# The first batch of a block-sparse attention and mixer kernel: a new order of loads, casts and weights, all-row mask products, and keys at the head of ScalarE's queue

## The chip, the core and the metric

The kernel runs on one NeuronCore of a Trainium2 chip. The metric is the device time of one execution in microseconds, read as the median of several executions. The profile is of one execution; its span leaves out some 1.8 us of the metered time. Names used below: TensorE (matrix products; "PE" in profile lines, "PEld" for its weight loads), VectorE ("DVE"), ScalarE ("ACT"), GpSimd ("POOL"), SyncE ("SP"; here it only issues DMAs). A trailing q (SPq, ACTq, POOLq) marks a DMA issue.

## The reference

Four batches, eight heads, 768 positions, head size 64. Attention with a block mask (blocks of 32: neighbours, first and last block, and three sampled key blocks for each query block), then a mixer:

```python
scores = scale * q @ k^T
mask = neighbour | first/last block | sampled blocks       # 24 x 24 blocks of 32
attn = softmax(where(mask, scores, -1e9)); x = attn @ v    # x: (4, 768, 512)
h = (x^T @ U) @ V                                          # rank 32
u = x + h^T
out = u + relu(u @ w_ch1) @ w_ch2                          # 512 -> 2048 -> 512
```

## The kernel before

Work goes in 16 pairs of heads; four pairs make a batch. A pair has nine units; a unit is a score product (`psc`), one 128x1024 exponential on ScalarE (`est`), and later the value products (`pav`). Batch 0 (pairs 0 to 3, 36 units) has no dense work to overlap with. From pair 4 on TensorE interleaves attention with the two dense products (`pt`, `pch`). In batch 0 the mask is carried inside the score product: 64 extra rows of `qa` hold a mask row per block, 64 extra rows of `ka` hold a one-hot pattern. The mask rows come from a small product, here called the mask product (`pm`).

The start, cut to what the argument touches:

```python
    keep(nc.vector.memset(zeros, 0.0))
    for h in (1, 0):
        keep(nc.vector.memset(ka[0][h][mrows[h], :], 0.0))
    keep(nc.vector.memset(cbd, 0.0))
    # ... (two more memsets)
    keep(nc.sync.dma_start(out=sbi[0:NB]...,  in_=sampled_blocks...))
    keep(nc.scalar.dma_start(out=small[0:NB], in_=small_dr.ap()))              # mask constants, NB = 24 rows
    keep(nc.sync.dma_start(out=qld[:, :, 0:TQ], in_=q0[:, :, 0:TQ]))
    keep(nc.scalar.dma_start(out=kld[:, :, 0:TK], in_=k0[:, :, 0:TK]))         # first keys
    # ... rest of q0, k0, identity, one-hot patterns
    vld = new_ld(0, "v")
    keep(nc.gpsimd.tensor_copy(out=vld[:, 0, 0, 0:1], in_=kld[:, 0, 0, 0:1]))  # a gate: v0 waits for the keys
    keep(nc.sync.dma_start(out=vld, in_=src_of("v", 0)))
    issue(1)                                                                   # q1, k1, v1, behind v0 on SyncE
    warm_pe(8)                                                                 # eight 128x512 products of zeros
    # ... VectorE: eq, cb, cbd from small and sampled_blocks
    def mask_mm(o, a, e):
        mm(o, cbd[0:NB].rearrange("z a c -> z (a c)"), small[0:NB, a:e], True, True)
```

What hangs on the units of batch 0, cut in the same way:

```python
WLOADS = ...((1, 3), (1, 5), (1, 7), (2, 0), (2, 3), (2, 5), (2, 7), (3, 0))   # w1 x4, then w2 x4, from GpSimd
# after unit 0 of pair 0, on SyncE:
#   for both heads: copy of the mask rows for the second buffer, one-hot pattern (64 rows) for it
#   V, V, U, then q2, k2
# at unit 6 of pair i, on GpSimd: casts of q and k of pair i+2, before the tails (which hold the casts xh and uh)
```

"Tails" are the mixer's first steps for a finished pair: `pa`, `ph`, the GpSimd cast `uh`, and TensorE's turning of it (`puT`).

The softmax here doesn't subtract the row's maximum and nothing guards it: scores larger than these inputs give would overflow.

## Time and profile before

| | before |
|---|---|
| time, median | 283.48 us (3 runs, 282.89 to 284.21) |
| profiled span | 281.8 us |
| first exponential starts | 7.26 us |
| 37th exponential ends | 45.44 us |
| first product with w1 starts | 47.98 us |
| ScalarE busy between first and 37th | 35.32 of 38.18 us |
| TensorE busy, 78 to 203 us | 124.54 of 125.00 us |

The page's first parts, engine totals and the clock row, look as if TensorE were the limit throughout:

```profile
PE 272.5 (97%) x3497; PEld 162.3 (58%) x3497; DVE 175.1 (62%) x285; ACT 177.5 (63%) x199; POOL 100.5 (36%) x132
...
PEclk9999999999999999999999999999999999999999
```

The split by stage says otherwise. Columns of these lines: stretch and its length, then busy time and instruction count of PE, PEld, DVE, ACT and POOL, then granted clock, DMA share, GB/s.

```profile
7.26:45.44 38.18, 34.86 (x489) 25.17 (x488) 25.25 (x54) 35.32 (x37) 25.53 (x39) 1.00 1.03 261
...
78.00:203.00 125.00, 124.54 (x1851) 75.57 (x1849) 93.33 (x137) 88.81 (x97) 57.12 (x66) 1.00 1.10 106
```

In the second stretch TensorE has half a microsecond to spare in 125. In the first, ScalarE ought to be the limit, as each unit has one exponential, but it idles 2.9 us. The timeline of ScalarE in that stretch shows where (start, length, what; x7 is a run of seven, and the bracket is the idle time before the run and what ended it):

```profile
7.26 6.90 ACT L494 ACTIVATE est<-psc 128x1024 f16<-128x1024 f32 x7 [0.54 <-PE psc L174]
14.49 4.69 ACT L494 ACTIVATE est<-psc 128x1024 f16<-128x1024 f32 x5 [0.33 <-PE psc L174]
...
23.95 2.94 ACT L494 ACTIVATE est<-psc 128x1024 f16<-128x1024 f32 x3 [0.51 <-PE psc L174]
28.26 17.18 ACT L494 ACTIVATE est<-psc 128x1024 f16<-128x1024 f32 x18 [1.38 <-PE psc L174]
46.28 1.94 ACT L494 ACTIVATE est<-psc 128x1024 f16<-128x1024 f32 x2 [0.84 <-PE psc L174]
```

The chain of waits through 5 to 60 us follows the late start at 28.26 back to its cause (start, length, what):

```profile
6.35 8.04 DMA vld<-in_v_dram
...
14.45 0.84 POOL vt L242
...
15.62 6.63 DMA vld<-in_v_dram
...
22.30 0.83 POOL vt L242
...
25.07 0.83 POOL kst L248
25.91 0.45 POOL uh L655
...
27.39 0.34 PE puT L707 x3
...
28.26 0.80 ACT est L494
```

v1 lands 8.0 us after its issue, GpSimd casts it, v2 can only then be issued and lands 6.6 us later, GpSimd's casts stand in a row behind it, uh among them, and TensorE's turning of uh is what the exponential waited for.

SyncE's timeline has the cause of the late q2 (L319 is v0; L233 at 6.35 is v1, at 14.46 q2; L1002 is U):

```profile
4.91 0.37 SPq L319 DMA_DIRECT2D vld<-in_v_dram  x1
...
6.35 0.47 SPq L233 DMA_DIRECT2D vld<-in_v_dram  x1
...
12.59 0.35 SPq L1002 DMA_DIRECT2D w2t<-in_moe_U_dram  x1
14.46 0.38 SPq L233 DMA_DIRECT2D qld<-in_q_dram  x1
```

q2, issued at 14.46, waited 1.4 us for v1 to land, though its buffer had been free since 5.5.

TensorE at the start:

```profile
0.99 3.59 PE L174 MATMUL warm<-m 128*128 128x512 f16 x8 [0.99 <-DVE m L286]
4.51 0.76 PE L174 MATMUL pm<-w1t,cbd 24*128 24x512 f16 x3
5.21 0.39 PE L174 MATMUL warm<-m 128*128 128x512 f16 x1
```

The first eight products are 0.43 us apart. The same products are 0.21 us apart from 5.8 us on; the two spacings are called half and full clock below. The three mask products (512, 512 and 256 columns) after 4.51 need 0.70 us in all to the next product's start. The profile's granted clock reads 1.00 over these 7.26 us.

### The profile page before, as it was taken

The numbers are of one execution on the slowest core, as the hardware profiler recorded it, in microseconds if no ns is written. First come the engines' busy times: TensorE is split into PE (matmuls) and PEld (weight loads), VectorE is DVE, ScalarE is ACT, GpSimd is POOL, SyncE is SP. The second block draws the span as 40 slices with busy tenths as digits, with TensorE's granted clock in tenths as the row PEclk, the third lists the DMA queues.
The fourth block names the chain that finished last, engine by engine and source line by source line (L and its number), as shares of the span: only waits on it lengthen the run. The fifth ranks groups of instructions, "written<-read, shape, count | busy, mean of one in ns | idle before, by whom it ended". The sixth has DMA issues, their size and how long they took to land.

```text
span 281.8 us, 8050 instructions
## 1 busy us (share of the span) xinstructions
PE 272.5 (97%) x3497; PEld 162.3 (58%) x3497; DVE 175.1 (62%) x285; ACT 177.5 (63%) x199; POOL 100.5 (36%) x132
## 2 busy tenths in 40 slices
PE   8997998999999999999999999999999999999995
PEld 3565775456566564656665555657565544655443
DVE  6765767797888878765967767784979541000112
ACT  4997997696969847595876657596868101654000
POOL 2379857205356646361614545361102020000000
PEclk9999999999999999999999999999999999999999
DMA  5989999993979999997794999993100313000112
GB/s 173 268 240 333 238 247 187 155 117 25 95 75 112 155 122 148 139 131 83 49 123 28 142 100 134 167 111 55 30 2 2 102 22 128 31 1 2 74 74 77
DMA packets 85716, 31.71 MB, mean 112 GB/s; under 512 B 75304, under 2 KB 83312, under 8 KB 85680
## 3 DMA queue, kind: packets, MB, share of 16 engines
q0 software_dynamic: 49728, 10.10, 47.7%
q1 hardware_dynamic: 35464, 20.85, 35.0%
q8 instruction: 27, 0.44, 0.6%
q10 hardware_dynamic: 488, 0.24, 0.3%
q14 instruction: 9, 0.07, 0.1%
HBM read 27.90 MB, written 6.29 MB: 121 GB/s over the span
## 4 chain that ended last, share of the span: by engine, by line
PE 79%; DMA 6%; ACT 6%; POOL 3%; issue 2%; DVE 1%; SPq 1%; ACTq 0%; POOLq 0%; DVEq 0%
PE pt L174 29%; PE pch L174 28%; PE pav L174 10%; PE psc L174 8%; ACT est L494 6%; DMA vld<-in_v_dram 5%; PE pa L174 2%; DMA kld<-in_k_dram 1%; POOL xh L594 1%; PE ph L174 1%; POOL uh L655 1%; POOL vt L242 1%; POOL w1t L434 0%; SPq L233 0%; DVE xh L537 0%
## 5 line engine op out<-in xcount | busy, mean ns | idle before, releaser
L494 ACT ACTIVATE est<-psc 128x1024 f16<-128x1024 f32 x144 | 142.5, 1028 | 42.0 <-PE psc L174 40.4
L174 PE MATMUL pt<-uT,w1t 64*128 64x384 f16 (+1 forms) x896 | 94.6, 324 | 0.5 <-ACT est L494 0.4
L174 PE MATMUL pch<-w2t,tT 64*128 64x512 f16 (+3 forms) x688 | 93.3, 372 | 0.2
L515 DVE TENSOR_TENSOR est<-est,m 128x1024 f16<-128x1024 f16 x108 | 78.7, 745 | 17.2 <-ACT est L494 16.0
L174 PEld LDWEIGHTS <-w1t 64*128 64x128 f16 (+1 forms) x896 | 46.7, 94 | 36.5 <-PE pt L174 6.7
L174 PEld LDWEIGHTS <-tT 64*128 64x128 f16 (+1 forms) x688 | 37.7, 95 | 38.5 <-PE pch L174 1.4
L732 ACT ACTIVATE tT<-pt 128x768 f16<-128x768 f32 (+1 forms) x48 | 36.8, 776 | 33.7 <-PE pt L174 33.7
L174 PEld LDWEIGHTS <-est 128*128 128x128 f16 x1152 | 41.4, 97 | 10.9 <-issue 5.1
L174 PE MATMUL pav<-vt,est 128*128 128x65 f16 x1152 | 44.4, 193 | 0.1
L594 POOL CAST xh<-xs 128x768 f16<-128x768 f32 x12 | 11.5, 955 | 86.5 <-DVE xs L585 55.9
L787 DVE TENSOR_TENSOR of<-xf,pch 128x1024 f32<-128x1024 f32 (+3 forms) x16 | 15.3, 954 | 43.5 <-PE pch L174 43.4
L174 PE MATMUL psc<-qT,kT 64*128 64x512 f16 (+1 forms) x288 | 40.8, 323 | 0.0
L680 POOL CAST uh<-xf 128x768 f16<-128x768 f32 x12 | 13.0, 1087 | 25.2 <-issue 12.9
L174 PE MATMUL psc<-qa,ka 128*128 128x512 f16 (+1 forms) x96 | 21.5, 326 | 0.3
L734 DVE TENSOR_SCALAR tT<-pt 128x768 f16<-128x768 f32 (+1 forms) x20 | 18.2, 916 | 4.6 <-PE pt L174 4.5
L174 PEld LDWEIGHTS <-kT 64*128 64x128 f16 x288 | 14.4, 94 | 11.0 <-DVE xs L585 0.2
L262 POOL DMA_DIRECT2D qst<-in_q_dram x20 | 16.3, 821 | 0.1
L262 POOL DMA_DIRECT2D vt<-in_v_dram x20 | 16.3, 822 | 0.0
L262 POOL DMA_DIRECT2D kst<-in_k_dram x20 | 16.3, 821 | 0.0
L583 DVE RECIPROCAL rcp<-pav 128x12 f32<-128x12 f32 x12 | 2.8, 233 | 16.0 <-PE pav L174 16.0
L585 DVE TENSOR_TENSOR xs<-pav,rcp 128x768 f32<-128x768 f32 x12 | 11.5, 958 | 1.2
L671 DVE TENSOR_TENSOR xf<-xs,ph 128x768 f32<-128x768 f32 x12 | 11.4, 950 | 1.3 <-PE ph L174 1.1
(68 smaller groups left out, 134.8 us busy)
## 6 DMA issues: line engine op xcount, KB each, us to landing
out_dram<-of SPq DMA_DIRECT2D x9, 512.0 KB, 3.7
vld<-in_v_dram SPq DMA_DIRECT2D x6, 384.0 KB, 8.0
w1t<-in_moe_w_ch_dram POOLq DMA_DIRECT2D x4, 512.0 KB, 10.7
w2t<-in_moe_w_ch_dram POOLq DMA_DIRECT2D x4, 512.0 KB, 18.4
qld<-in_q_dram SPq DMA_DIRECT2D x5, 384.0 KB, 6.2
kld<-in_k_dram SPq DMA_DIRECT2D x5, 384.0 KB, 7.2
qst<-in_q_dram POOLq DMA_DIRECT2D x20, 96.0 KB, 3.9
kst<-in_k_dram POOLq DMA_DIRECT2D x20, 96.0 KB, 4.8
```

Source lines behind the costliest of these rows:

```text
L174: ins = nc.tensor.matmul(out, lhsT, rhs, start=start, stop=stop, skip_group_check=loose)
L242: nc.gpsimd.tensor_copy(out=vts[b % 2][:, 2 * hp : 2 * hp + 2, :, 0:D], in_=ld)
L262: keep(nc.gpsimd.dma_start(out=o[:, h], in_=src_of(nm, i)[:, h]))
L494: keep(nc.scalar.activation(out=est, in_=psc, func=AF.Exp, scale=0.125))
L515: keep(nc.vector.tensor_tensor(out=o, in0=o, in1=m, op=ALU.mult))
L585: nc.vector.tensor_tensor(out=xs.rearrange("p (c j) (h d) -> p c (j h) d", c=2, h=2), in0=pv[:, :, :, 0:D], in1=rcp[:, :, :, None].broadca ...
L594: keep(nc.gpsimd.tensor_copy(out=xh, in_=xs))
L671: nc.vector.tensor_tensor(out=u.rearrange("p (c j) n -> p c j n", c=2), in0=xs.rearrange("p (c j) n -> p c j n", c=2), in1=ph[:, :, 0:HS]. ...
L680: keep(nc.gpsimd.tensor_copy(out=uh, in_=u))
L732: keep(nc.scalar.activation(out=o, in_=i, func=AF.Relu))
L734: keep(nc.vector.tensor_scalar_max(out=o, in0=i, scalar1=0.0))
L787: nc.vector.tensor_add(out=of, in0=xfs[b][:, sc : sc + nsc, n0:n1], in1=pch)
```

## The change

Its intent: bring the loads, casts and weights of batch 0 into the order in which they are needed, start the keys first, and run the mask products over all 128 rows. The core of the diff (cut where marked):

```diff
     keep(nc.vector.memset(zeros, 0.0))
+    keep(nc.vector.memset(small, 0.0))
@@ issues at the start
-    keep(nc.scalar.dma_start(out=small[0:NB], in_=small_dr.ap()))
     keep(nc.sync.dma_start(out=qld[:, :, 0:TQ], in_=q0[:, :, 0:TQ]))
     keep(nc.scalar.dma_start(out=kld[:, :, 0:TK], in_=k0[:, :, 0:TK]))
+    keep(nc.scalar.dma_start(out=small[0:NB], in_=small_dr.ap()))
@@ mask_mm
-            cbd[0:NB].rearrange("z a c -> z (a c)"),
-            small[0:NB, a:e],
+            cbd.rearrange("z a c -> z (a c)"),
+            small[:, a:e],
@@ GpSimd, after the casts of pair 0 (the memsets of the ones column move to the very start)
-    for vt in vts:
-        keep(nc.gpsimd.memset(vt[:, :, :, D : D + 1], 1.0))
+    for h in range(2):
+        hot_rows(nc.gpsimd, 1, h, D)          # was on SyncE, between the mask-row copies
@@ SyncE after unit 0 of pair 0
-   V, V, U, q2, k2
+   q2, U, k2, V, V
@@ weights
-            ((1, 3), (1, 5), (1, 7), (2, 0), (2, 3), (2, 5), (2, 7), (3, 0))
+            ((1, 3), (1, 4), (2, 3), (2, 4), (HP, 0), (HP, 2), (HP, 4), (HP, 6))
@@ casts of the next pair, now after the tails
-        if u == 6:
-            cast(i + 2, "q")
-            cast(i + 2, "k")
-        if u == 8:
-            cast(i + 2, "v")
         for _ in range(...): tails.popleft()()
+        if u == 7:
+            cast(i + 2, "q")
+        if u == 8:
+            cast(i + 2, "k")
+        if u == 0 and i > 1:
+            cast(i + 1, "v")
```

Also, pair 2 is turned one unit earlier and its q is cast before U.

More of the change, by code (lines that the diff above doesn't have):

```diff
@@ L314 @@
     keep(nc.scalar.activation(out=dummy, in_=zeros[:, 0:1], func=AF.Exp))
+    for vt in vts:
+        keep(nc.gpsimd.memset(vt[:, :, :, D : D + 1], 1.0))
     vld = new_ld(0, "v")
@@ L989, in at_unit @@
                     mask_rows("dve", h, pm2[:, 0, 0:QB], QA, S)
+                for nm, o, pt, t in (("q", qa[0], pq, TQ), ("k", ka[0], pk, TK)):
+                    for h in range(2):
+                        half_copy(nc.vector.tensor_copy, o, h, pt, t, T)
+                for h in range(2):
                     keep(
@@ L994, in at_unit @@
                     )
-                    hot_rows(nc.sync, 1, h, D)
-                for nm, o, pt, t in (("q", qa[0], pq, TQ), ("k", ka[0], pk, TK)):
-                    for h in range(2):
-                        half_copy(nc.vector.tensor_copy, o, h, pt, t, T)
-                for h in range(2):
-                    keep(nc.sync.dma_start(out=mvld[h * R : h * R + R], in_=moe_V))
+                issue(2, "q")
                 keep(
@@ L1005, in at_unit @@
                 )
-                issue(2, "qk")
+                issue(2, "k")
+                for h in range(2):
+                    keep(nc.sync.dma_start(out=mvld[h * R : h * R + R], in_=moe_V))
                 cast(1, "q")
@@ L1014, in at_unit @@
             if u == 6:
+                cast(2, "q")
                 cast_U()
-                cast(2, "q")
                 cast(2, "k")
@@ L1034, in at_unit @@
             WLOADS[i, u]()
-        at = u - 2 if i == 1 else u - 1
-        if at in range(4):
-            turn_part(i + 1, "qk"[at // 2], at % 2)
-        if u == 6:
-            cast(i + 2, "q")
-            cast(i + 2, "k")
-        if u == 8:
-            cast(i + 2, "v")
+        if u in (1, 2, 3, 4):
+            turn_part(i + 1, "qk"[(u - 1) // 2], (u - 1) % 2)
         for _ in range({0: 1, 5: 2, 6: 1, 7: 1}.get(u, 0)):
@@ L1069, in unit_sides @@
             turn_dma(i + 1, "k")
+        if (i, u) in WLOADS:
+            WLOADS[i, u]()
         if u in (3, 5, 7):
@@ L1104 @@
             flush_value()
+            cast(HP + 1, "v")
         if gi == 1:
```

## The prediction

> **What bounds it now.** Batch 0 (first 45 us, 36 units) runs at ScalarE's pace: one 128x1024 exponential per unit; in the undisturbed stretch (timeline, 28.3 to 45.4 us) 18 take 17.2 us, 0.955 us each. After about 48 us TensorE is the limit: 79.7 us busy of 80 between 120 and 200 us (windows). So whatever brings stage two forward reaches the end undiluted; nothing else counts.
>
> Stage one loses time. The timeline shows ScalarE idle for 0.33, 0.29, 0.51 and 1.38 us before exponentials between 14 and 28 us, then 0.84 at 46.3. The chain of waits explains them: 26.7% of 5 to 60 us is value loads (v of pair 1: 8.0 us from issue; pair 2: 6.6), then GpSimd casts that queue behind them, then TensorE waiting for GpSimd's uh cast (0.40+0.65 us near 27). Again later: the cast of k of pair 5 waits 2.8 us for a load that took 17.4 us, delays uh, and TensorE waits at 44.8.
>
> **What the change does.**
> - SyncE's queue: [...] Before, U waits for k1 (issued 12.6), q2 for v1 (14.5, though its buffer was free at 5.5). After, the two 96 KB pattern loads leave that queue and q2 leads U and V: q2 should issue near 8.5, k2 near 9, about 5 us earlier.
> - w2 (4 x 512 KB) moves from 30-37 us to the first units of pair 4, near 40-48. In 25 to 45 us the software queue takes 79.7% of the DMA engines, the hardware queue 29.6%. [...] Loads of pairs 4 and 5 should land in under 10.
> - GpSimd: uh now precedes the casts of the next pair (0.83 us each). The two added pattern issues (0.6 us each on SyncE) fit the 0.8 us idle before the first v cast plus the 0.53 us memset that moves earlier.
> - Start: a 128x408-word memset (0.38 us for 128x384), the keys' load 0.6 us earlier, the mask constants' 0.6 later. The mask products start when the eight warming products end (4.5 us), not when cbd is ready (3.4); that slack hides both. All-row products stream the same columns.
> - TensorE's order changes only in when pair 2's q and k are turned (one unit earlier); ScalarE's compute order not at all.
>
> **Sum.** Exponential gaps: 2.5 us, of which 0.4 stay (q2 and q3 turns have less slack behind GpSimd). Transition at 44 to 47 us: 0.7. Start: 0.1. Stage two gives back 0.2: q6/k6 loads stand behind two or three w2 pieces in the software queue; needed near 71 us, first w2 use near 79. Net 2.7 us of 283.5, 1%.
>
> Predicted 280.8 us, 279.4 to 282.6 eight times in ten. Faster by over 2%: 0.03; within: 0.95; slower: 0.02.
>
> **What would show it.** ScalarE's gaps between 14 and 28 us shrink from 2.5 to under 0.7; the 36th exponential ends near 42 (was about 44.5); first product with w1 near 45 (was 48.0); q2 issued before 9.5; k5 lands in under 10 us; w2 landed before 70; TensorE's idle from 50 to 200 us unchanged (under 1 us); first exponential near 7.2.
>
> **What would make it wrong.** k6 arriving after 65 us, so pair 6's scores stall (up to 2 us); GpSimd's order putting q2, U, k2 behind a late v1; late mask constants moving the first exponential past 7.6; pair 5's transposing DMAs, now meeting w2, taking over 15 us.

What the trace of before shows is that U waited 1.9 us for k1 to land and q2 1.4 us for v1, and that k5 took 17.4 us to land where the quickest load of keys took 3.3. The sum came to 2.1 + 0.7 + 0.1 - 0.2 = 2.7 us. That k5 would land in under 10 us once w2 had moved, on which part of the transition's 0.7 rests, is the author's estimate.

## The result

The changed kernel takes 280.78 us (median of 4 runs, 280.53 to 280.88) against 283.62 (4 runs, 282.89 to 284.21). The ratio is 0.990, 95% interval 0.9875 to 0.9924. Ratios here are the mean time of one kernel's fast runs over the mean of the other's of the same rounds, so not quite the ratio of the medians quoted. The change is about 1% faster, and the interval is clear of 1.

```profile
PE 272.3 (98%) x3497; PEld 162.6 (58%) x3497; DVE 175.4 (63%) x286; ACT 177.0 (63%) x199; POOL 101.7 (36%) x134
...
PEclk9999999999999999999999999999999999999999
```

The split by stage, with boundaries at the same events as before (same columns):

```profile
8.19:43.20 35.01, 34.63 (x499) 25.47 (x497) 25.53 (x55) 34.88 (x37) 22.61 (x35) 1.00 0.90 243
...
75.00:200.00 125.00, 124.54 (x1855) 75.58 (x1853) 93.33 (x138) 88.68 (x97) 56.99 (x66) 1.00 1.08 106
```

ScalarE's exponentials, before in six runs with gaps, are now two:

```profile
8.19 35.01 ACT L497 ACTIVATE est<-psc 128x1024 f16<-128x1024 f32 x37 [0.54 <-PE psc L174]
43.42 1.94 ACT L497 ACTIVATE est<-psc 128x1024 f16<-128x1024 f32 x2 [0.22 <-PE psc L174]
```

SyncE (L322 is v0; L233 at 5.36 is v1, at 9.29 q2; L1004 is U):

```profile
3.29 0.37 SPq L322 DMA_DIRECT2D vld<-in_v_dram  x1
...
5.36 0.48 SPq L233 DMA_DIRECT2D vld<-in_v_dram  x1
...
9.29 0.55 SPq L233 DMA_DIRECT2D qld<-in_q_dram  x1
9.89 0.49 SPq L1004 DMA_DIRECT2D w2t<-in_moe_U_dram  x1
```

v0 goes 1.6 us earlier, v1 1.0, q2 5.2. TensorE at the start:

```profile
0.99 3.59 PE L174 MATMUL warm<-m 128*128 128x512 f16 x8 [0.99 <-DVE m L286]
4.78 1.25 PE L174 MATMUL pm<-w1t,cbd 128*128 128x512 f16 x3 [0.20 <-DVE cbd L353]
5.82 0.63 PE L174 MATMUL warm<-m 128*128 128x512 f16 x1
6.25 0.50 PE L267 MATMUL pturn<-id,qst 128*128 128x128 f16 x4
```

Here the mask products are still 0.40 and 0.43 us apart (half clock) and need 1.04 us in all, where they needed 0.70 before. The sum of the two profiles, worked out from the event times:

| stretch | before | after | difference |
|---|---|---|---|
| start to first exponential | 7.26 | 8.19 | +0.93 |
| first exponential to end of 37th | 38.18 | 35.01 | -3.17 |
| from there to first product with w1 | 2.54 | 1.92 | -0.62 |
| from there to the end of the span | 233.82 | 233.88 | +0.06 |
| span | 281.8 | 279.0 | -2.8 |

The total is as predicted, but it is not the sum that was predicted: the start lost 0.9 where 0.1 was to be won. That is what the experiments went after.

### The profile page after: what moved, and what is told of

The parts are those of the page before. It is cut to its first block, busy times and chain, and to the rows that moved or that the text cites. A ratio compares the mean times of both kernels' runs of the same rounds, so it can differ in the third digit from the quotient of the medians.

```text
span 279.0 us, 8049 instructions
## 1 busy us (share of the span) xinstructions
PE 272.3 (98%) x3497; PEld 162.6 (58%) x3497; DVE 175.4 (63%) x286; ACT 177.0 (63%) x199; POOL 101.7 (36%) x134
## 4 chain that ended last, share of the span: by engine, by line
PE 91%; ACT 3%; DVE 2%; POOL 1%; DMA 1%; issue 1%; DVEq 0%; ACTq 0%; POOLq 0%
PE pt L174 30%; PE pch L174 28%; PE psc L174 13%; PE pav L174 13%; ACT est L497 3%; PE pa L174 2%; PE ph L174 1%; POOL xh L597 1%; DMA w1t<-small_const 1%; PE pturn L267 1%; PE pmk L174 1%; PE warm L174 0%; PE pm L174 0%; PE puT L710 0%; DVE xh L540 0%
```

## The experiments

Twelve kernels ran, in three calls; the kernels of one call shared a chip and its runs of the kernel before (medians 283.72, 283.21 and 283.60 us). All were correct. "Change" below is the changed kernel.

| kernel | what it is | median (range, runs) | ratio to before, 95% |
|---|---|---|---|
| change | | 280.78 (280.53-280.88, 4) | 0.9900 (0.9875-0.9924) |
| old_start | change, start undone (ones column stays early) | 282.40 (280.58-282.56, 6) | 0.9937 (0.9917-0.9958) |
| w2_early | change, weights at old units | 280.58 (280.40-280.78, 4) | 0.9887 (0.9874-0.9899) |
| old_queue | change, SyncE's old order | 281.24 (280.72-281.60, 4) | 0.9908 (0.9894-0.9922) |
| start_alone | before, start of the change | 282.02 (281.57-282.48, 5) | 0.9933 (0.9918-0.9948) |
| keys_only | change, 24-row mask products | 282.77 (280.87-283.16, 6) | 0.9955 (0.9920-0.9990) |
| rows_first | change, constants lead again, all rows | 281.38 (280.66-282.42, 6) | 0.9924 (0.9896-0.9953) |
| warm_24 | change, warming products over 24 rows | 282.35 (281.89-282.78, 4) | 0.9962 (0.9925-0.9998) |
| consts_pool | change, constants from GpSimd's queue | 281.11 (280.73-282.84, 6) | 0.9926 (0.9894-0.9959) |
| before_again | before, unchanged | 283.59 (282.60-284.55, 6) | 0.9997 (0.9970-1.0023) |
| rows_alone | before, all-row mask products | 283.46 (282.48-284.37, 6) | 0.9997 (0.9967-1.0026) |
| old_casts | change, casts before uh | 281.32 (280.95-282.12, 6) | 0.9920 (0.9896-0.9944) |
| consts_sync | change, constants lead SyncE's queue | 280.44 (280.16-281.29, 6) | 0.9890 (0.9866-0.9913) |

### First call: which part makes the gain

**old_start**, the change with the start put back (no clearing of `small`, the old issue order, 24 rows; the memsets of the ones column stay at the very start):

```diff
-    keep(nc.vector.memset(small, 0.0))
+    keep(nc.scalar.dma_start(out=small[0:NB], ...))   # again ahead of the keys
-            cbd..., small[:, a:e]
+            cbd[0:NB]..., small[0:NB, a:e]
```

> The changed kernel with the start of before: mask constants lead ScalarE's queue again, no clearing of the pattern rows, mask products over 24 rows. Theory S (the start costs what the two traces show: first exponential at 8.19 us after, 7.26 before): first exponential at 7.2 to 7.5, stage one and the rest unchanged, time 279.9 (0.9 below the change's 280.8). Rival R [...]: first exponential anywhere from 7.2 to 8.2, time within 0.3 of 280.8 on the mean.

(Rival R puts the late full clock of the mask products down to chance and not to the edit.)

Measured: 282.40, with one run of six at 280.58. Theory S fell: the start of before is slower in the changed kernel, by 1.6 us of medians, not faster. Against w2_early, which has the change's start and ran on the same chip, it is 1.8 us, and the two intervals are apart. Rival R fell as well: the mean is not equal, and in the profile the first exponential came at 9.54 us, outside its 7.2 to 8.2.

**w2_early**, the change with the old list of units for the weights:

```diff
-            ((1, 3), (1, 4), (2, 3), (2, 4), (HP, 0), (HP, 2), (HP, 4), (HP, 6))
+            ((1, 3), (1, 5), (1, 7), (2, 0), (2, 3), (2, 5), (2, 7), (3, 0))
```

> The changed kernel with the eight weight loads at their old units. Theory D (w2 moved out of stage one is what lets the late loads land): k of pair 5 lands in over 14 us again, GpSimd holds uh back, TensorE waits near 42 us, and 0.6 to 1.5 us come back: 281.4 to 282.3. Rival Q (the order of SyncE's queue does it nearly all): within 0.3 of 280.8.

Measured: 280.58. Theory D fell; moving w2 out of batch 0 is worth nothing here. k of pair 5 took 13.3 us to land with w2 in its old place and 13.8 us in the change; both are in time, as TensorE never waits for uh in either.

**old_queue**, the change with SyncE's old order:

```diff
-        hot_rows(nc.gpsimd, 1, h, D)     # GpSimd
+        hot_rows(nc.sync, 1, h, D)       # SyncE, between the mask-row copies
-   q2, U, k2, V, V
+   V, V, U, q2, k2
```

> The changed kernel with SyncE's old order: pattern loads in its queue, both halves of V and U ahead of q2 and k2. Theory Q: q2 is issued near 14 us again, ScalarE's gaps between 14 and 28 us return in good part, 282.0 to 283.0 (1.2 to 2.2 us back). Theory D: under 0.5 us back.

Measured: 281.24. That is 0.44 over the 280.8 from which the expectation counted, so inside theory D's number, although w2_early had just refuted theory D's mechanism; over w2_early on the same chip it is 0.66, between the two theories. q2 was issued late again, at 13.47, and the profile has one gap in the stretch, 0.82 us; there TensorE's turning of q2 waits 1.0 us for GpSimd's cast:

```profile
7.80 10.57 ACT L495 ACTIVATE est<-psc 128x1024 f16<-128x1024 f32 x11 [0.74 <-PE psc L174]
19.18 24.68 ACT L495 ACTIVATE est<-psc 128x1024 f16<-128x1024 f32 x26 [0.82 <-PE psc L174]
```

So the mechanism of theory Q is there and is well under the size expected. The intervals of old_queue and w2_early just overlap; the gap in the trace is the firmer evidence.

**start_alone**, before with the first hunks of the change and the early ones column:

```diff
+    keep(nc.vector.memset(small, 0.0))
-    keep(nc.scalar.dma_start(out=small[0:NB], ...))      # ahead of the keys
+    keep(nc.scalar.dma_start(out=small[0:NB], ...))      # behind the keys
-            cbd[0:NB]..., small[0:NB, a:e]
+            cbd..., small[:, a:e]
```

> Before with the start of the change alone: clearing of the pattern rows, keys first, all-row mask products, the ones columns set early. Theory S: first exponential near 8.2, 0.5 to 1.0 us slower than before (284.1 to 284.6). Rival R: within 0.3 of before[...].

Measured: 282.02, ratio 0.9933: 1.7 us faster than before, though its first exponential came at 8.23, a microsecond later. Both theories fell. v0 was issued at 3.28 (4.91 before), q1 at 4.43 (5.33), v1 at 5.89 (6.35), and of the 3.35 us of idle gaps that the profile of before shows ahead of ScalarE's exponentials (0.33, 0.29, 0.51, 1.38, 0.84) two stay, with 0.22 us later:

```profile
8.23 15.41 ACT L495 ACTIVATE est<-psc 128x1024 f16<-128x1024 f32 x16 [0.54 <-PE psc L174]
24.14 2.94 ACT L495 ACTIVATE est<-psc 128x1024 f16<-128x1024 f32 x3 [0.51 <-PE psc L174]
27.73 16.95 ACT L495 ACTIVATE est<-psc 128x1024 f16<-128x1024 f32 x18 [0.64 <-PE psc L174]
```

The keys' lead opens the gate to v0, q1, k1 and v1 sooner, and that pays in the load-bound stage one of before. In start_alone v1, q2, k2 and v2 landed at 12.7, 16.1, 18.5 and 20.1 us, each earlier than in the profiles of before, before_again and rows_alone (13.0, 17.6, 18.6 and 20.6 at the earliest), and its chain of waits from 5 to 50 us shows no load of q, k or v, where value loads are 32.6% of the same stretch before. The early ones column, the other part of this edit, is ruled out as a cause by the trace: GpSimd is idle for 0.56 us before it casts v0 at 8.34, room for the 0.53 us memset at its old place.

### Second call: rows or order

The profile of old_start has TensorE at half clock until about 9.7 us (the four warming products from 6.73 on are 0.43 us apart), where that of start_alone has full clock from about 6.3 (the four from 6.74 on are 0.21 us apart). The last slow product of old_start, 0.43 us before the next start:

```profile
9.29 0.60 PE L174 MATMUL warm<-m 128*128 128x512 f16 x1
9.72 0.29 PE L267 MATMUL pturn<-id,qst 128*128 128x128 f16 x2
```

Besides the order of their loads, the two starts differ in the three mask products before that: in start_alone they run over 128 rows and follow 0.44 us of idle time, in old_start they run over 24 rows and no idle time precedes them that the profile shows. Theory H says that products over few rows do less to raise the clock than the same products over all rows.

**keys_only**, the change with 24-row mask products and no clearing; the keys still lead:

```diff
-    keep(nc.vector.memset(small, 0.0))
-            cbd..., small[:, a:e]
+            cbd[0:NB]..., small[0:NB, a:e]
```

> The changed kernel with mask products over 24 rows again and no clearing; the keys still lead ScalarE's queue. Theory H [...]: most runs 1.0 to 1.8 us over the change's 280.8, a few equal to it, and in the profile of a late one products of 512 columns 0.43 us apart beyond 7 us and a first exponential after 9 us. Rival K (the undone start cost 1.6 us because the keys, and with them the gated loads of v0, q1, k1, v1, came 1 to 1.6 us later): within 0.4 of 280.8, since the keys lead here.

Measured: two runs at 280.87 and 281.16, four at 282.50 to 283.16. The profile is of a slow one. TensorE, from its timeline:

```profile
4.80 1.24 PE L174 MATMUL pm<-w1t,cbd 24*128 24x512 f16 x3 [0.21 <-DVE cbd L352]
...
7.01 1.91 PE L174 MATMUL warm<-m 128*128 128x512 f16 x4
8.71 1.06 PE L174 MATMUL psc<-qa,ka 128*128 128x512 f16 x2
9.57 0.60 PE L174 MATMUL warm<-m 128*128 128x512 f16 x1
9.99 0.29 PE L267 MATMUL pturn<-id,qst 128*128 128x128 f16 x2
```

The four warming products start at 7.01 and the score product after them at 8.71: 0.43 us each, where the change has 0.21 (6.69 to 7.55). The first exponential starts at 9.81. The keys' lead did not help: rival K fell. Theory H held in kind (a slow cluster, a fast one, and a late profile as described), but three of the four slow runs lie 2.2 to 2.4 us over 280.8, more than its 1.8. The clusters are about 2 us apart where the whole change is 2.8, so a comparison of a few runs of two kernels can be misled by them.

**warm_24**, the change with the eight warming products over 24 rows:

```diff
-    mm(warm..., zeros,       zeros[:, None, :]...)        # in the eight at the start
+    mm(warm..., zeros[0:24], zeros[0:24, None, :]...)
```

> The changed kernel with its eight warming products over 24 rows instead of 128, same columns and count; result unchanged. Theory H: these do not lift the clock, the mask products always start at half clock (0.43 us apart for 512 columns), [...] first exponential after 8.5 us, 0.5 to 1.5 us slower than 280.8. Rival (rows do not matter to the clock): within 0.3 of 280.8, first exponential 7.8 to 8.3.

Measured: every run between 281.89 and 282.78, and a first exponential at 9.26. The clock rises about 8.3 us in the profile (about 6.5 in the change's), and the mask products, the lone warming product and the first turns are at half clock:

```profile
3.52 1.05 PE L174 MATMUL warm<-m 24*128 24x512 f16 x2
5.13 1.25 PE L174 MATMUL pm<-w1t,cbd 128*128 128x512 f16 x3 [0.55 <-DVE cbd L353]
...
6.60 0.63 PE L267 MATMUL pturn<-id,qst 128*128 128x128 f16 x4
...
7.24 1.56 PE L174 MATMUL warm<-m 128*128 128x512 f16 x4
8.63 0.59 PE L174 MATMUL psc<-qa,ka 128*128 128x512 f16 x2
```

Same instructions, same columns, same count, fewer rows: 1.6 us slower in the median than the change, whose runs were of another call. With four slow runs of four here and four fast ones of four there, this is the most direct evidence for theory H; the clock itself was seen in one profile.

**rows_first**, the change with the constants leading ScalarE's queue again but all-row products (the constants padded to 32 rows, GpSimd clears the other 96, so no load waits for a clearing):

```diff
-    keep(nc.vector.memset(small, 0.0))
-    keep(nc.scalar.dma_start(out=small[0:NB], ...))      # behind the keys
+    keep(nc.scalar.dma_start(out=small[0:32], ...))      # ahead of the keys, padded
+    keep(nc.gpsimd.memset(small[32:64], 0.0)); keep(nc.gpsimd.memset(small[64:P], 0.0))
```

> The changed kernel with the mask constants leading ScalarE's queue as before, but all-row mask products: the constants are padded to 32 rows, GpSimd clears the other 96, so their load waits for nothing. Theory H: within 0.5 of 280.8, first exponential 7.2 to 8.3, no half-clock products after 6.8 us. Rival K: 281.8 to 282.5, as with the whole start undone.

Measured: 281.38, between the two theories' numbers (theory H's ended at 281.3). The clock was up by 4.2 us (the three mask products need 0.54 us to the next start), the first exponential came at 7.17, and yet four small gaps were back (0.29, 0.36, 0.24 and 0.22 us before later exponentials). v0 was issued late again, and TensorE's waits name it:

```profile
PE pturn L270 <- POOL qst L251: 0.6, 1, 0.6
```

A start that is a microsecond earlier gave part of itself back to late loads. This trace suggests that both parts are needed, rows for the clock and keys for the loads; the interval of the ratio (0.9896 to 0.9953) overlaps the change's, so the loss in time is not firm.

**consts_pool**, a candidate with the constants issued from GpSimd's queue:

```diff
-    keep(nc.vector.memset(small, 0.0))
-    keep(nc.scalar.dma_start(out=small[0:NB], ...))
+    keep(nc.gpsimd.dma_start(out=small[0:32], ...))      # first of GpSimd's work
+    keep(nc.gpsimd.memset(small[32:64], 0.0)); keep(nc.gpsimd.memset(small[64:P], 0.0))
```

> Candidate: the changed kernel with keys leading ScalarE's queue and the mask constants (padded to 32 rows) loaded from GpSimd's queue at once, GpSimd clearing the other 96 rows, so the constants wait for no clearing and no other issue. If the constants' landing (3.94 us in the changed kernel) is what starts the mask products late: cbd ready by 4.3, mask products straight after the warming products at 4.5, 0.2 to 0.5 us faster than 280.8. Otherwise, if the load lands no sooner from that queue: 280.6 to 281.2.

Measured: 281.11, the second of the two cases, so the candidate missed; the spread is wide (280.73 to 282.84), and the profile is of the slowest run. The constants were issued at 1.23 us and VectorE could use them at 5.03, 3.8 us later (in the change 24 rows took 2.5 us from ScalarE's queue; here it is 32 rows, and both loads run beside the first loads of q and k). TensorE sat idle for 1.38 us before the mask products at 5.97, and the clock rose only near 9.9 (products until 9.78 are 0.43 us apart) although these products have all rows. In this one profile the clock came as late after an idle gap as after the 24-row products of the others (9.7 us in old_start, 10.0 in keys_only).

### Third call: control, parts in before, and a better version

**before_again**, the unchanged kernel, no edit:

> The kernel before, unchanged, as a second look at its start and a control of the timing. Theory H: its time is spread over some 2 us[...]; if this profile is of a late one, TensorE runs at half clock to 8 us or beyond and the first exponential comes after 9 us, against 7.26 in the first profile, while the 37th exponential's end moves by less than that start (part is absorbed by waits for loads that are there anyway). Ratio to before 1.00 within 0.4%.

Measured: ratio 0.9997. The profile is again of an early clock (first exponential at 7.18), so the case that I wanted to see, before with a late clock, was not seen; that part of the expectation is open. Its gaps fall elsewhere than in the first profile, yet their sum, 3.46 us (1.68, 0.51, 1.05, 0.22), is about the same as the first one's 3.35:

```profile
20.35 3.97 ACT L494 ACTIVATE est<-psc 128x1024 f16<-128x1024 f32 x4 [1.68 <-PE psc L174]
24.82 2.94 ACT L494 ACTIVATE est<-psc 128x1024 f16<-128x1024 f32 x3 [0.51 <-PE psc L174]
28.80 17.18 ACT L494 ACTIVATE est<-psc 128x1024 f16<-128x1024 f32 x18 [1.05 <-PE psc L174]
```

A late load may show as a wait at one place in one execution and at another in the next.

**rows_alone**, before with all-row mask products alone:

```diff
-    keep(nc.scalar.dma_start(out=small[0:NB], ...))
+    keep(nc.scalar.dma_start(out=small[0:32], ...))      # same place, padded
+    keep(nc.gpsimd.memset(small[32:64], 0.0)); keep(nc.gpsimd.memset(small[64:P], 0.0))
-            cbd[0:NB]..., small[0:NB, a:e]
+            cbd..., small[:, a:e]
```

> Before with all-row mask products alone (constants padded to 32 rows, GpSimd clears the other 96; constants still lead ScalarE's queue, SyncE's order, casts and weights as before). If the full rows alone make the gain of the start (start_alone was 1.7 us faster than before): 281.7 to 282.3. If the keys' earlier landing, which releases v0, q1, k1, v1, makes it: 283.2 to 283.8. Both in part: in between.

Measured: 283.46, ratio 0.9997. Full rows alone do nothing that could be measured for before (the interval leaves room for up to 0.9 us); the gain of start_alone is by elimination that of the keys' lead (the keys alone in before were not run). Both profiles of before caught an early clock, and so does this one (0.70, 0.65 and 0.63 us from the first mask product to the product after the three), so rows had little to win in them. One caution: the keys landed somewhat later here, so v1 was issued at 6.64 and not at 6.35.

**old_casts**, the change with the casts of the next pair back ahead of the tails:

```diff
+        if u == 6: cast(i + 2, "q"); cast(i + 2, "k")
+        if u == 8: cast(i + 2, "v")
         for _ in range(...): tails.popleft()()
-        if u == 7: cast(i + 2, "q")
-        if u == 8: cast(i + 2, "k")
-        if u == 0 and i > 1: cast(i + 1, "v")
```

> The changed kernel with GpSimd's casts of the next pair back ahead of uh. Theory C (the order of casts kept uh late): TensorE waits for GpSimd's uh cast, 0.3 to 1.0 us in all, 281.1 to 281.9. Rival (with the loads early, GpSimd has the slack and the order does nothing): within 0.3 of 280.8.

Measured: 281.32; the profile has one gap, and the waits of TensorE name uh again with 0.2 us (GpSimd starts uh at 24.96 here, at 23.45 in the change). Theory C holds in kind; the intervals of this ratio and the change's overlap, so the size, about half a microsecond, is uncertain.

```profile
26.85 16.95 ACT L497 ACTIVATE est<-psc 128x1024 f16<-128x1024 f32 x18 [0.65 <-PE psc L174]
```

**consts_sync**, a candidate with the constants first in SyncE's queue and the keys first in ScalarE's:

```diff
-    keep(nc.vector.memset(small, 0.0))
-    keep(nc.scalar.dma_start(out=small[0:NB], ...))      # behind the keys
+    keep(nc.sync.dma_start(out=small[0:32], ...))        # first of SyncE's issues, padded to 32 rows
+    keep(nc.gpsimd.memset(small[32:64], 0.0)); keep(nc.gpsimd.memset(small[64:P], 0.0))
```

> Candidate: the changed kernel with the mask constants (padded to 32 rows) leading SyncE's queue while the keys lead ScalarE's; GpSimd clears the other 96 rows. The constants should land near 2.8 us, cbd be ready by 3.5, so TensorE goes from the warming products to full-row mask products without the 0.2 to 0.4 us wait: first exponential 7.1 to 8.0[...], 0.2 to 0.6 us faster than the change. A miss would be 280.7 or more: q0's load, now 0.5 us later, then bounds the first turns.

Measured: 280.44, the lowest median of all, 0.3 us below the change's; the interval of its ratio (0.9866 to 0.9913) covers the change's 0.990, so that it beats the change is not shown. The mask products began at 4.11 us, but q0's load, issued 0.4 us later than in the change, then bound the first turns (TensorE waits 1.0 us for VectorE's cast of it), and the first exponential came at 8.08. That it is faster than before is clear.

## Why the prediction was right, and where it was not

The predicted 280.8 us was measured as 280.78. What carried it was the frame, and that held: batch 0 is bound by the exponentials, everything after it by TensorE, so a gain in batch 0 arrives at the end undiluted. The first product with w1 moved by 2.86 us and the end by 2.8. ScalarE is now busy 34.88 of the 35.01 us of its stretch, so this stage has little more than a tenth of a microsecond left, its start apart.

The terms of the sum:

- **Exponential gaps, predicted 2.1 won.** The stretch won 3.17. The 0.4 us of gaps that were to stay did not: no gap is left in that stretch, and the small gaps inside the runs shrank too (37 exponentials took 0.946 us each, where the undisturbed stretch of before had 0.955). Under-sized.
- **Transition, predicted 0.7.** Measured 0.62. But the second profile of before has only 0.22 us there and the same span, so this is one place where a late load may strike, and not a term of its own.
- **Start, predicted 0.1 won ("that slack hides both").** Wrong in sign: 0.93 lost in the profile pair. The constants landed at 3.94 us, 2.5 us after their issue, so cbd was ready at 4.7 and not at 4.0, and the mask products ran at half clock, which I had not considered although the trace of before shows both spacings. The clearing of `small` is not what made the constants late: keys_only has none and VectorE could use them at 4.06 there, at 4.04 in the change; the place behind the keys is. "All-row products stream the same columns" is true (at half clock the three products took 1.25 us over 128 rows in the change, 1.24 over 24 in keys_only) and beside the point: keys_only and warm_24, with full clock from about 10.0 and 8.3 us where the change has it from about 6.5, indicate that the rows bear on when the clock rises. Nor does the start alone fix when it rises: w2_early, with the change's start, had full clock from about 4.8 us (its mask products need 0.55 us to the next start, where the change's need 1.04) and had its first exponential at 7.81.
- **SyncE's queue.** q2 was to be issued near 8.5 and was at 9.29, k2 near 9 and was at 10.47. I gave this mechanism most of the gain (1.2 to 2.2 us in the expectation for old_queue); undoing it costs 0.66 us against w2_early. What I costed least, the keys' earlier landing, was worth most in before (start_alone, 1.7 us): I had written "the keys' load 0.6 us earlier" and not followed it through the gate to v0, q1, k1 and v1, though v1 was the head of my own chain.
- **w2 moved away.** k5 was to land in under 10 us and took 13.8; with w2 in its old place it took 13.3. So the step from w2's transfers to the late k5 failed; the 3.3 us to which its 17.4 was compared was also that of a 128 KB load, where the best 384 KB load of keys before took 3.7. w2 itself landed in time (the last piece issued at 49.5, landed after 12.2 us, first used near 78.5).
- **Stage two, predicted 0.2 lost.** Measured 0.06. k6 landed near 59 us, before the 65 that I feared.

So the total was right to 0.1 us by luck: two errors cancelled, gaps under-sized by about a microsecond, start wrong by about a microsecond. Removing the parts one at a time from the change costs 1.6 (start), 0.5 (queue) and 0.5 us (casts) of medians, and w2 nothing; these are small against the spread of some kernels, and they need not add up, since late loads and a late clock hide each other. Three small parts were undone by no run from the change: the early ones column, the earlier turning of pair 2, and its q cast before U.

That hiding also reconciles start_alone with old_start. In before, loads bind, so the first exponential may come a microsecond later and nothing is lost, while earlier loads are won. An earlier v1 alone is not enough: in before_again v1 landed at 13.0, 1.4 us earlier than in the first profile, and the span is the same, as q2 and k2 landed later. In the change, loads bind no more, so a late clock shows at once: old_start and keys_only have a slow cluster near 282.5 and 283 and a fast one near 281. That explanation for before is argued from gaps and landings; its late-clock case was not caught.

## What to carry to other kernels

When several streams of loads hang on one gate, follow a moved issue through the gate to everything behind it; here 1.6 us at the gate (in the kernel before) were worth more than 4 to 5 us for a load further back (in the change). What each is worth depends on what else is late. Look at the rows of the products that run while TensorE is still at half clock, and at the gaps between them: in the changed kernel 24 rows instead of 128 cost 1.6 us of medians in the eight warming products (warm_24) and 2.0 in the three mask products (keys_only, two of whose six runs were as fast as the change), and after an idle gap of 1.38 us full clock came only near 9.9 us in the one profile of it (consts_pool). In before, rows alone gained nothing measurable (rows_alone). And check a prediction term by term: a total that is right to 0.1 us had two terms wrong by a microsecond each.
